# Seven block products in all twelve chunks of tile 7, with the sums of x in two alternating fields

## The chip, the cores and the metric

The kernel runs on one core of a Trainium2 chip. The metric is the device time of one execution in microseconds. Matrix products run on TensorE (PE in the profile), elementwise work on VectorE (DVE), ScalarE (ACT) and GpSimd (POOL); SyncE (SP) issues most DMAs. Each engine works through its own queue in order.

## The reference

Two stages: attention over pooled keys and values, then a gated feed-forward layer on its output.

```python
k_p = k.reshape(B, H, Sp, 8, D).mean(axis=3)          # B=8, H=8, Sp=72, D=64
v_p = v.reshape(B, H, Sp, 8, D).mean(axis=3)
scores = scale * np.matmul(q, k_p.transpose(0, 1, 3, 2))
scores = scores - np.max(scores, axis=-1, keepdims=True)
attn = np.exp(scores)
attn = attn / (np.sum(attn, axis=-1, keepdims=True) + 1e-09)
x = np.matmul(attn, v_p)                              # as 4608 tokens x 512
g = x @ w_gate                                        # 512 x 1536
out = (g * sigmoid(g) * (x @ w_val)) @ w_out          # 1536 x 512
```

## The kernel before

The 4608 tokens of x are cut into nine tiles of 512, numbered 0 to 8, and the 1536 hidden columns into twelve chunks of 128. For every tile and chunk TensorE makes gate and value products into PSUM (gv), ACT and DVE make tanh and products of them (hf), and TensorE adds the chunk's part of the output into four banks (acc, `project`, L956, twelve matmuls). Every operand is held as a high and a low half in 16 bits, so each product is three matmuls.

A chunk's gate and value products come in two forms. The plain form (`side`, L923, lines L927 to L929) takes 24 matmuls of 512 columns. The other form (`product`, L1090, line L1109) splits x and the weights of a chunk into blocks and makes seven block products from sums of blocks, 42 matmuls of 256 columns. It needs the sums of the weights (`fast_weights`, L1014) and the sums of x (`fast_x`, L1045), which DVE, POOL and ACT make beforehand. READY (L65) says for each tile how many chunks, from chunk 0 on, take the seven products; the others of a tile come first, in plain form. MADE (L66) and LATE (L67) say in which tile the sums of a chunk's weights are made.

`fast_x` works in two halves of 256 tokens. Of each half it adds the high and low parts (L1057), makes four differences in the tile `fx` (L1064), casts them to the high halves (ACT, L1077) and subtracts to get the low halves (L1083). A tile whose twelve chunks all take the seven products keeps the first block sum in its own x (L985 to L986); the other tiles keep it in `first`. The other six go to one of two fields of the tensor `area` (`halves_of`, L980): the number of tiles past SOLO (L70), modulo two, says which. The second field lies on the second of the two buffers for softmax numbers (`halves`, L192), so from tile SOLO on `soft` (L816) uses the first buffer alone, and lets a piece wait until TURNS has gone by, in the planner's count, since the transposition of the piece before (L817, L841).

The attention of later tiles runs between the chunks of a tile, in pieces of up to 128 tokens: scores (L631, L632), row maximum and subtraction (L641, L642), exponentials and casts (L653, L713 to L722), POOL's low halves (L727, L730), a transposing DMA (L734), value products (L755, L756), a division (L760), two halves of x (L882, L885) and a transposing DMA into x (L890). Where each step stands on its engine is decided when the program is built, by a planner: `slot` (L1170) lets through what fits beside TensorE's work by its own counts of time. The order on every engine is then fixed. `begin_fast` (L1404) forces what is still missing for a tile's sums before it issues the first product.

CROSS (L69) names the tiles whose first chunk begins inside the last chunk of the tile before (L1475). Then `begin_fast` issues product 5 (which reads the first block sum) and product 1 for the next tile before the output matmuls of the last chunk are all done.

Of the kernel before, what the change touches and what calls it, by code (L numbers as in the profile page):

```python
# [61 lines left out]

ROOM = (3410, 3290)
FAST = 10
READY = (0,0,5,7,9,9,9,9,12)  # L65
MADE = (0,5,7,9,9,9,9,11)  # L66
LATE = {8:(11,)}  # L67
DV = 5
CROSS = (8,)  # L69
SOLO = 7  # L70
CAME = 6000
URGE = (0, 0)
FAST_ROOM = (3500, 1350), (2550, 2210), (1250, 1050), (950, 180), (3350, 800), (1760, 4190), (2900, 5200)
# [27 lines left out]
def attention_then_swiglu(  # L101
# [711 lines left out]
    def soft(t):  # L813

        i, off, b, s0, m = t["at"]
        half, sc = halves[t["me"] % 2 if now["tile"] < SOLO else 0], t["sc"]  # L816
        while now["tile"] >= SOLO and now["pe"] < last["turned"]:  # L817
            yield 0, 0
# [158 lines left out]
    def ready(i):  # L977
        return READY[min(i, len(READY) - 1)]

    def halves_of(i):  # L980

        s = max(0, i - SOLO) % 2
        a = area.bitcast(F16)[:, s * 2 * SLOT : (s + 1) * 2 * SLOT]
# [30 lines left out]
    def fast_weights(c):  # L1014

        yield 1400, 0
        f = xp.tile([P, 2 * DM], F32, name="fw", tag="f", bufs=1)
        g_h, g_l = (a[:, c].rearrange("p i j f -> p (i j f)") for a in (wgv_h, wgv_l))
        nc.vector.tensor_add(f, g_h, g_l)
        a11, a12, a21, a22 = (f[:, i * HT : (i + 1) * HT] for i in range(4))  # L1020
        nc.gpsimd.tensor_add(a22, a21, a22)
        nc.gpsimd.tensor_sub(a21, a11, a21)
        nc.gpsimd.tensor_sub(a11, a22, a11)
        nc.gpsimd.tensor_sub(a12, a12, a11)
        spend("P", 3000, "V")
        yield from settle("P")
        yield 0, 1200
        outs = []
        for places, wgv in zip(sums_of(c), (wgv_h, wgv_l)):
            own = wgv[:, c, 1, :HJ].rearrange("p j f -> p (j f)")  # L1030
            outs.append([*places, (own, slice(3 * HT, 4 * HT))])
        for o, cs in outs[0]:
            nc.scalar.copy(o, f[:, cs])
        for o, cs in outs[1]:
            hi, his = next(q for q in outs[0] if q[1].start <= cs.start < q[1].stop)
            for at in range(cs.start, cs.stop, TILE):
                e = min(cs.stop, at + TILE)
                nc.gpsimd.tensor_sub(
                    o[:, at - cs.start : e - cs.start], f[:, at:e],
                    hi[:, at - his.start : e - his.start],  # L1040
                )
        spend("P", 2600, "A")
        yield from settle("P")
# [46 lines left out]
    def product(o, k, c, i, begin):  # L1090

        x, (rest, one) = xs[i], halves_of(i)
        if k in (3, 6, 7):
            ws = sum_of(c, {3: 1, 6: 0, 7: 2}[k])
        for j in range(HJ):
            w = [a[:, j] for a in ws] if k in (3, 6, 7) else {
                1: (wgv_h[:, c, 0, j], wgv_l[:, c, 0, j]),
                2: (wgv_h[:, c, 0, HJ + j], wgv_l[:, c, 0, HJ + j]),
                4: (wgv_h[:, c, 1, HJ + j], wgv_l[:, c, 1, HJ + j]),
                5: (wgv_h[:, c, 1, j], wgv_l[:, c, 1, j]),  # L1100
            }[k]
            if k in (1, 2, 3):
                rows, cs = {1: (j, slice(0, HT)), 2: (HJ + j, slice(0, HT)), 3: (HJ + j, slice(HT, TILE))}[k]
                xh, xl = x["h"][:, rows, cs], x["l"][:, rows, cs]
            else:
                n = {7: 0, 4: 1, 6: 2}.get(k)
                xh, xl = (a[:, j] for a in one) if n is None else (a[:, j, n] for a in rest)
            for n, (a, b) in enumerate(((w[0], xh), (w[0], xl), (w[1], xh))):
                nc.tensor.matmul(  # L1109
                    o, a, b, start=begin and j + n == 0, stop=j == HJ - 1 and n == 2,  # L1110
                    skip_group_check=True,
                )
                now["pe"] += 109
# [31 lines left out]
    def join(line, g, t=None):  # L1145
        lines[line].append({"g": g, "t": t, "need": next(g)})
# [222 lines left out]
    def hidden_tiles():  # L1369
# [28 lines left out]
        def low_of(eng, hf, hh, n):  # L1398
            hl = hp.tile([P, TILE], BF16, name="hl")
            eng.tensor_sub(hl[:, :n], hf, hh[:, :n].bitcast(F32))  # L1400
            spend(*(("V", 700) if eng is nc.vector else ("P", 1200)), "A")
            return hl

        def begin_fast(k, c):  # L1404
# [11 lines left out]
            product(t["x"], 1, c, k, False)  # L1416
            if c == ready(k) - 1 and SOLO < k + 1 < len(tiles) and ready(k + 1) < NCH and not left[k + 1]:
                summed.add(k + 1)
# [21 lines left out]
        for i, (_, n, _) in list(enumerate(tiles))[1:]:  # L1440
# [15 lines left out]
            if i > 1 and n_fast < NCH and i not in summed:  # L1456
                join("extra", fast_x(i), ("x", i))
                if len(lines["extra"]) > 2:
                    lines["extra"].insert(1, lines["extra"].pop())
            for c in LATE.get(i, ()):  # L1460
                join("extra", fast_weights(c), ("w", c))
# [5 lines left out]
            for at_step, c in enumerate(order):  # L1467
# [5 lines left out]
                if not ends[1] and order[at_step + 1] < n_fast:  # L1473
                    soon = i, order[at_step + 1]
                elif ends[1] and i + 1 in CROSS:  # L1475
                    soon = i + 1, 0
# [41 lines left out]
                else:  # L1518
# [10 lines left out]
                    hl = low_of(nc.gpsimd if i == 1 else nc.vector, h, hh, n)  # L1529
                    if c < MADE[min(i, len(MADE) - 1)]:  # L1530
                        join("extra", fast_weights(c), ("w", c))
# [72 lines left out]
```

## Time and profile before

| | |
|---|---|
| median of 3 runs | 920.8 us (919.76 to 925.22) |
| profiled execution | 923.62 us |
| its span | 921.8 us |
| mean granted TensorE clock | 0.994 of full speed |
| TensorE busy | 886.5 us, 96% of the span |

The span is the time from the first to the last recorded instruction of the profiled execution. Times inside it are given from its start. A row of a timeline has the start, the duration, the engine, the line in the kernel, the operation with what it writes and reads, the shape, how many instructions are merged, and in brackets how long the engine had been idle before and what ended it. The granted clock is a share of full speed, where 1.00 is 2.4 GHz and 0.50 is 1.2 GHz.

### The profile page before, as it was taken

The numbers are of one execution on the slowest core, as the hardware profiler recorded it, in microseconds if no ns is written. First come the engines' busy times: TensorE is split into PE (matmuls) and PEld (weight loads), VectorE is DVE, ScalarE is ACT, GpSimd is POOL, SyncE is SP. The second block draws the span as 40 slices with busy tenths as digits, with TensorE's granted clock in tenths as the row PEclk, the third lists the DMA queues.
The fourth block names the chain that finished last, engine by engine and source line by source line (L and its number), as shares of the span: only waits on it lengthen the run. The fifth ranks groups of instructions, "written<-read, shape, count | busy, mean of one in ns | idle before, by whom it ended". The sixth has DMA issues, their size and how long they took to land.

```text
span 921.8 us, 16917 instructions
## 1 busy us (share of the span) xinstructions
PE 886.5 (96%) x6428; PEld 588.3 (64%) x6519; DVE 646.1 (70%) x1156; ACT 515.7 (56%) x1084; POOL 458.7 (50%) x516
## 2 busy tenths in 40 slices
PE   3889999999999999999999999999999999999997
PEld 3776555454555575567657765776577757777775
DVE  6899997777767679676867777677755585634233
ACT  2677763385456554756476655655647555444343
POOL 3656785498656944776375342543125416114111
PEclk9899999999999999999999999999999999999999
DMA  9866733256444732863285335642333322201001
GB/s 329 264 204 252 255 92 91 77 160 174 84 117 89 202 87 50 203 156 80 53 203 161 77 71 163 169 94 40 84 78 75 76 69 40 31 1 46 1 1 47
DMA packets 161681, 104.76 MB, mean 114 GB/s; under 512 B 119360, under 2 KB 148032, under 8 KB 160064
## 3 DMA queue, kind: packets, MB, share of 16 engines
q1 hardware_dynamic: 159872, 84.81, 36.8%
q10 hardware_dynamic: 1728, 18.88, 5.5%
q8 instruction: 51, 0.84, 0.4%
q14 instruction: 30, 0.25, 0.1%
HBM read 67.63 MB, written 9.44 MB: 84 GB/s over the span
## 4 chain that ended last, share of the span: by engine, by line
PE 74%; DVE 17%; issue 2%; ACT 2%; DMA 2%; POOL 1%; SPq 0%; ACTq 0%; DVEq 0%; POOLq 0%
PE gv L1109 30%; PE acc L963 24%; PE gv L929 5%; PE gv L927 5%; PE gv L928 5%; DVE mixed L244 3%; DVE wgv_l L278 2%; DVE ws L233 2%; DVE hf L945 1%; DVE hf L951 1%; PE ps L631 1%; DMA k<-k_rows 1%; PE ps L416 1%; DVE sc L642 1%; PE ps L632 1%
## 5 line engine op out<-in xcount | busy, mean ns | idle before, releaser
L1400 POOL TENSOR_TENSOR hl<-hf,hh 128x512 bf16<-128x512 f32 x71 | 92.9, 1309 | 201.2 <-ACT hh L1391 201.2
L941 ACT ACTIVATE hf<-gv,un 128x512 f32<-128x512 f32 (+1 forms) x111 | 74.9, 675 | 162.2 <-PE gv L1109 104.3
L963 PE MATMUL acc<-hl,wo_h 128*128 128x512 bf16 (+1 forms) x435 | 161.4, 373 | 2.0
L945 DVE SCALAR_TENSOR_TENSOR hf<-hf,gv 128x512 f32<-128x512 f32 (+1 forms) x111 | 74.4, 670 | 115.4 <-ACT hf L941 115.3
L927 PE MATMUL gv<-x,wgv_h 128*128 128x512 f16 (+1 forms) x408 | 149.7, 367 | 1.9 <-DVE hf L945 1.6
L929 PE MATMUL gv<-x,wgv_l 128*128 128x512 f16 (+1 forms) x408 | 149.7, 367 | 1.6 <-DVE wgv_l L278 1.6
L928 PE MATMUL gv<-x,wgv_h 128*128 128x512 f16 (+1 forms) x408 | 149.6, 367 | 0.0
L963 PE MATMUL acc<-hh,wo_h 128*128 128x512 f32 (+1 forms) x444 | 130.3, 415 | 0.0
L614 POOL TENSOR_TENSOR box<-qt,box 64x512 f16<-64x512 f32 (+1 forms) x60 | 66.3, 1104 | 104.9 <-ACT box L613 91.5
L963 PE MATMUL acc<-hb,wo_l 128*128 128x512 bf16 x307 | 117.4, 382 | 0.4
L1109 PEld LDWEIGHTS <-mixed 128*128 128x128 f16 x1044 | 101.2, 98 | 25.3 <-issue 0.9
L1109 PEld LDWEIGHTS <-wgv_h 128*128 128x128 f16 x960 | 93.0, 98 | 33.7 <-issue 2.0
L1391 ACT CAST hh<-hf 128x512 fp32r<-128x512 f32 x72 | 44.4, 617 | 118.9 <-DVE hf L951 118.7
L1109 PE MATMUL gv<-area,mixed 128*128 128x256 f16 x696 | 95.0, 273 | 0.0
L1109 PE MATMUL gv<-x,wgv_h 128*128 128x256 f16 x528 | 93.0, 273 | 0.0
L951 DVE SCALAR_TENSOR_TENSOR hf<-gv,un,hf 128x512 f32<-128x512 f32 (+1 forms) x87 | 63.2, 727 | 37.6 <-PE gv L1109 34.4
L963 PEld LDWEIGHTS acc<-hh,wo_h 128*128 128x128 f32 x444 | 76.5, 189 | 14.1 <-ACT hh L1391 0.3
L963 PEld LDWEIGHTS <-wo_l 128*128 128x128 bf16 x444 | 43.2, 97 | 52.0 <-issue 26.2
L1109 PE MATMUL gv<-x,wgv_l 128*128 128x256 f16 x264 | 72.0, 273 | 0.0
L929 PEld LDWEIGHTS <-wgv_l 128*128 128x128 f16 x408 | 39.9, 98 | 45.7 <-DVE wgv_l L278 2.9
L928 PEld LDWEIGHTS <-wgv_h 128*128 128x128 f16 x408 | 39.9, 98 | 39.9 <-issue 2.4
L927 PEld LDWEIGHTS <-wgv_h 128*128 128x128 f16 x408 | 39.9, 98 | 37.5
(205 smaller groups left out, 1896.4 us busy)
## 6 DMA issues: line engine op xcount, KB each, us to landing
ws<-w_all ACTq DMA_DIRECT2D x12, 1536.0 KB, 6.7
qt<-q_twice SPq DMA_DIRECT2D x48, 256.0 KB, 3.1
out_t<-ob SPq DMA_DIRECT2D x36, 256.0 KB, 2.5
in<-k_rows SPq DMA_DIRECT2D x12, 576.0 KB, 4.8
in<-q_rows SPq DMA_DIRECT2D x12, 576.0 KB, 4.8
in<-v_main SPq DMA_DIRECT2D x12, 512.0 KB, 4.8
in<-v_rest SPq DMA_DIRECT2D x12, 512.0 KB, 5.0
qt<-q_rows SPq DMA_DIRECT2D x8, 256.0 KB, 4.9
```

Source lines behind the costliest of these rows:

```text
L244: nc.vector.scalar_tensor_tensor(out=wf.bitcast(U32), in0=wf.bitcast(U32), scalar=3, in1=chunks[c]["low"], op0=ALU.logical_shift_left, op1 ...
L614: nc.gpsimd.tensor_sub(o[rows], qt[rows], o[rows])
L927: nc.tensor.matmul(o, wh, x["h"][:, j, a:e], start=(j == 0), stop=False)
L928: nc.tensor.matmul(o, wh, x["l"][:, j, a:e], start=False, stop=False)
L929: nc.tensor.matmul(o, wl, x["h"][:, j, a:e], start=False, stop=(j == NJ - 1))
L941: nc.scalar.activation(hf, gate, AF.Tanh, scale=un[:, c, 0:1])
L945: nc.vector.scalar_tensor_tensor(out=hf, in0=hf, scalar=1.0, in1=gate, op0=ALU.add, op1=ALU.mult)
L951: nc.vector.scalar_tensor_tensor(out=out, in0=val, scalar=un[:, c, 2:3], in1=hf, op0=ALU.mult, op1=ALU.mult)
L963: nc.tensor.matmul(acc[j][:, a:e], w[:, c, j * P : (j + 1) * P], h[:, :n], start=begin and at < NJ, stop=end and w is wo_up,)
L1109: nc.tensor.matmul(o, a, b, start=begin and j + n == 0, stop=j == HJ - 1 and n == 2, skip_group_check=True,)
L1391: nc.scalar.copy(hh[:, :n], hf)
L1400: eng.tensor_sub(hl[:, :n], hf, hh[:, :n].bitcast(F32))
```

## The change

Six constants change. Tile 7 takes seven products in all twelve chunks, as tile 8 does (READY). The sums of weight chunks 9 and 10 are made in tile 6 instead of tile 7 (MADE), those of chunk 11 in tile 7 instead of tile 8 (LATE). Tile 7 begins inside the last chunk of tile 6 (CROSS). SOLO goes from 7 to 6: the sums of x of tile 7 go to the second field and those of tile 8 to the first, and the softmax numbers have one buffer from tile 6 on.

```diff
-READY = (0,0,5,7,9,9,9,9,12)
-MADE = (0,5,7,9,9,9,9,11)
-LATE = {8:(11,)}
+READY = (0,0,5,7,9,9,9,12,12)
+MADE = (0,5,7,9,9,9,11,11)
+LATE = {7:(11,)}
 DV = 5
-CROSS = (8,)
-SOLO = 7
+CROSS = (7,8)
+SOLO = 6
```

On TensorE, where tile 7 starts, the last output matmuls of chunk 7 of tile 6 and what follows them. In both programs x_7737 is x of tile 7, and hl and hb are operands of the output matmuls. Before:

```order
L963 LDWEIGHTS wo_l_110
L963 MATMUL acc3_7904<-hb_8858,wo_l_110 128x512
L963 LDWEIGHTS wo_h_109
L963 MATMUL acc3_7904<-hl_8865,wo_h_109 128x512
L927 LDWEIGHTS wgv_h_107 [waits DMAHW1_49,DMAHW0_49]
L927 MATMUL gv0_8930<-x_7737,wgv_h_107 128x512 [waits PE_49]
L928 LDWEIGHTS wgv_h_107
L928 MATMUL gv0_8930<-x_7737,wgv_h_107 128x512
```

Now:

```order
L963 LDWEIGHTS wo_l_110
L963 MATMUL acc3_7904<-hb_8746,wo_l_110 128x512
L963 LDWEIGHTS wo_h_109
L963 MATMUL acc3_7904<-hl_8753,wo_h_109 128x512
L1109 LDWEIGHTS wgv_h_107 [waits DMAHW3_49,DMAHW0_49]
L1109 MATMUL gv1_8891<-x_7737,wgv_h_107 128x256 [waits Activation_49]
L1109 LDWEIGHTS wgv_h_107
L1109 MATMUL gv1_8891<-x_7737,wgv_h_107 128x256 [waits DVE_49]
```

The first matmul that reads x of tile 7 waited for its DMAs and for a bank of PSUM; it is now one of the block products, and waits for ACT's cast and the next one for DVE's subtraction.

On DVE, the sums of x of tile 7 (fx). Before, the first half's stood after the last products of tile 6 (un_8927 holds factors of tile 7, mt_8946 those of tile 8), the second half's further down:

```order
L951 SCALAR_TENSOR_TENSOR hf_8885<-gv2_8797,un_7719,hf_8885 128x512 [waits DVE_49,PE_49]
L1446 TENSOR_TENSOR un_8927<-p2w_113,mt_7738 128x36
L1057 TENSOR_TENSOR fx_8938<-x_7737 128x2x256 x2
L1064 TENSOR_TENSOR fx_8938<-fx_8938 128x2x128 [waits DVE_49] x4
L908 TENSOR_SCALAR mt_8946<-p2s_121 128x1
```

Now the second half's sums, ahead of the gate of the last chunk of tile 6 (hf_8879 is that chunk's; sc_8295 is the last piece of attention of tile 7, sc_8872 the next piece, of tile 8):

```order
L945 SCALAR_TENSOR_TENSOR hf_8791<-hf_8791,gv0_8725 128x512 [waits Activation_49]
L1492 TENSOR_TENSOR gv1_8686<-gv1_8686,rs_8715 128x256 [waits Activation_49]
L885 SCALAR_TENSOR_TENSOR box_1466<-sc_8295,r_7748,box_1466 64x512 [waits DVE_49]
L951 SCALAR_TENSOR_TENSOR hf_8791<-gv1_8686,un_7719,hf_8791 128x512 [waits DVE_49,PE_49]
L1435 TENSOR_TENSOR gv0_8832<-gv2_8792,rs_8822 128x256 [waits PE_49,Activation_49]
L641 TENSOR_REDUCE mx_8873<-ps_8863 128x4 [waits PE_49]
L642 TENSOR_TENSOR sc_8872<-ps_8863,mx_8873 128x288 [waits DVE_49]
L1057 TENSOR_TENSOR fx_8880<-x_7737 128x2x256 [waits DMAHW3_49,DMAHW0_49]
L1057 TENSOR_TENSOR fx_8880<-x_7737 128x2x256
L1064 TENSOR_TENSOR fx_8880<-fx_8880 128x2x128 [waits DVE_49] x4
L1083 TENSOR_TENSOR x_7737<-fx_8880,x_7737 128x2x128 [waits Activation_49]
L1083 TENSOR_TENSOR area_120<-fx_8880,area_120 128x6x128 [waits Activation_49]
```

All steps of that half now stand in one run, between the scores of the next piece and the gate of the last chunk.

On ACT, a piece's softmax numbers in tile 6. Before, in the second buffer (area):

```order
L941 ACTIVATE hf_8796<-gv0_8754,un_7719 128x512 [waits PE_49,Pool_49]
L1488 COPY gv1_8689<-gv1_8689 128x256 [waits PE_49]
L1424 COPY rs_8827<-gv2_8797 128x256
L713 CAST area_120<-sc_8712 128x8x64 [waits DMAHW4_49,Activation_49]
L1429 COPY gv0_8837<-gv2_8797 128x256 [waits DVE_49]
```

Now in the first (half), as for the piece before it:

```order
L941 ACTIVATE hf_8685<-gv0_8635,un_7719 128x512 [waits PE_49,Pool_49]
L1488 COPY gv2_8591<-gv2_8591 128x256 [waits PE_49,Activation_49]
L1424 COPY rs_8715<-gv1_8686 128x256
L713 CAST half_123<-sc_8515 128x8x64 [waits DMAHW6_49,Activation_49,Pool_49]
L1429 COPY gv0_8725<-gv1_8686 128x256 [waits DVE_49]
```

The cast's place in the chunk is the same; the DMA that it waits for is now that of the piece just before it.

## Rows read from the trace of the kernel before

**Rows 1.** The page, part 1: busy time, share of the span, instructions.

```profile
PE 886.5 (96%) x6428; PEld 588.3 (64%) x6519; DVE 646.1 (70%) x1156; ACT 515.7 (56%) x1084; POOL 458.7 (50%) x516
```

**Rows 2.** Stretches, PE alone: us, PE busy (matmuls), clock, DMA share, GB/s.

```profile
640.00:735.00 95.00, 94.35 (x749) 1.00 0.34 76
```

**Rows 3.** Waits of PE from 640 to 921 us: us, times, longest.

```profile
PE gv L1109 <- DVE hf L951: 0.2, 1, 0.2
```

**Rows 4.** Timeline of PE, a plain chunk of tile 6 and its neighbours.

```profile
657.95 0.20 PE L631 MATMUL ps<-box 128*128 128x72 f16 x1
...
658.20 0.38 PE L927 MATMUL gv<-x,wgv_h 128*128 128x512 f16 x1
...
663.39 0.38 PE L1109 MATMUL gv<-first,wgv_h 128*128 128x256 f16 x2
```

**Rows 5.** Chain that ended last, merged: start, us, what.

```profile
749.42 2.67 PE acc L963 x12
...
822.68 2.62 PE gv L1109 x24
```

**Rows 6.** Timelines of DVE, then ACT, tile 6, around a 64-token piece.

```profile
710.86 0.69 DVE L945 SCALAR_TENSOR_TENSOR hf<-hf,gv 128x512 f32<-128x512 f32 x1 [1.99 <-ACT hf L941]
711.47 0.43 DVE L1492 TENSOR_TENSOR gv<-gv,rs 128x256 f32<-128x256 f32 x1
...
715.14 1.14 DVE L885 SCALAR_TENSOR_TENSOR box<-sc,r,box 64x512 f16<-64x512 f32 x1
716.95 0.46 DVE L641 TENSOR_REDUCE mx<-ps 128x4 f32<-128x288 f32 x1 [0.66 <-PE ps L632]
717.44 0.46 DVE L642 TENSOR_TENSOR sc<-ps,mx 128x288 f32<-128x288 f32 x1
...
710.14 0.69 ACT L941 ACTIVATE hf<-gv,un 128x512 f32<-128x512 f32 x1 [1.43 <-PE gv L1109]
```

**Rows 7.** DMAs into x, issue to landing: at 716 us (at 693 alike); all thirty.

```profile
x<-box SPq DMA_TRANSPOSE x1, 2.6
...
DMA to landing us min/median/max: 2.6/3.4/6.3
```

**Rows 8.** Timelines of DVE, then ACT: sums of x of tile 8; differences of tile 7.

```profile
802.57 1.29 DVE L1057 TENSOR_TENSOR fx<-x 128x512 f32<-128x512 f16 x2
804.71 1.79 DVE L1064 TENSOR_TENSOR fx<-fx 128x256 f32<-128x256 f32 x4
808.68 0.84 DVE L1083 TENSOR_TENSOR x<-fx,x 128x256 f16<-128x256 f32 x1 [0.61 <-ACT x L1077]
...
736.05 2.88 DVE L1064 TENSOR_TENSOR fx<-fx 128x256 f32<-128x256 f32 x4
...
808.25 0.40 ACT L1077 CAST x<-fx 128x256 f16<-128x256 f32 x1
```

**Rows 9.** PE's timeline at three gaps; stretches around them (columns of rows 2).

```profile
20.69 0.16 PE L213 MATMUL ps<-wm,ones 128*128 128x2 bf16 x1 [2.85 <-ACT wgv_h L255]
...
32.61 3.22 PE L416 MATMUL ps<-vr,shapes 128*128 128x128 f32 x16 [1.88 <-DVE p2s L218]
...
478.93 0.20 PE L755 MATMUL ps<-box,pt 128*128 128x64 f16 x1 [1.39 <-DMA pt<-half]
...
19.50:20.00 0.50, 0.00 (x0) 0.60 0.68 207
26.00:27.00 1.00, 1.00 (x9) 0.79 0.67 221
33.00:34.00 1.00, 1.00 (x8) 0.63 1.40 305
36.50:37.00 0.50, 0.50 (x10) 0.83 1.58 272
474.00:479.00 5.00, 3.62 (x25) 1.00 0.69 119
```

**Rows 10.** Transposing DMAs of the softmax numbers (L734): issue to landing, all.

```profile
DMA to landing us min/median/max: 2.8/4.4/6.8
```

## The prediction

> **What bounds the kernel now.** I read the page first: TensorE (PE) is busy 96% of the span, VectorE (DVE) 70%, ScalarE (ACT) 56%, GpSimd (POOL) 50% [rows 1]. Such a share is an average, so I went on to the stage that the change touches, tiles 6 and 7, from about 640 to 830 us. There the table by stretches gives PE 94.35 of the first 95.00 us at the full clock [rows 2], and the list of waits from 640 us to the end holds a single wait of PE on another engine, 0.2 us long [rows 3]. In this stage everything else is hidden beside TensorE. Two things follow: a matmul that goes is gained in full, and a wait that is put in front of TensorE is lost in full.
>
> **What is removed.** Three chunks of tile 7 (9, 10 and 11) change from the plain form to the seven products. The plain form is 24 matmuls of 512 columns. Eight score matmuls start at 657.95 and end with the first plain matmul at 658.20; from there to the next kind at 663.39 the 24 take 5.19 us [rows 4]. The new form is 42 matmuls of 256 columns; 24 of them take 2.62 us, 0.109 each, so 42 take 4.58. The twelve output matmuls are the same in both, 2.67 us [rows 5]. The gain is 0.61 us a chunk, **1.8 us** for three. TensorE is bound there, so nothing gives it back.
>
> **What is added: a wait where tile 7 starts.** Before, tile 7 opened with plain chunks, which need x of tile 7 alone; its sums (first half and second) were made under them. Now the last chunk of tile 6 is followed at once by product 5 of tile 7, whose moving operand is a sum of x over all 512 tokens. So TensorE's own row for it waits for an ACT cast and then for a DVE subtraction of the second half of the sums, and these wait for the last 64-token piece of attention. I count from E, the end of that piece's value matmuls.
>
> TensorE after E: 42 products (4.58 us), 15 output matmuls (15 x 2.67/12 = 3.34) and eight score matmuls (0.25 [rows 4]), so it reaches product 5 at E+8.2. The scores are done three output matmuls earlier, at E+7.5.
>
> The piece's own way: division and scaling go at once, but its low half (L885) stands on DVE behind the chunk's tanh product and the sum of L1492. The tanh waits for 3 output matmuls and 18 products, so it starts at about E+2.8; from tanh to L945 is 0.72, then 0.69, 0.43 and L885 at 0.75 to 1.14: E+5.4 to 5.8 [rows 6]. The transposing DMA of such a 64-row piece took 2.6 us in tile 6 [rows 7], so x is complete at E+8.0 to 8.4.
>
> But DVE has something else ahead of the sums: the row maximum and the subtraction of the next piece's first scores. They wait for the scores at E+7.5, start at about E+7.7 (0.2 for the hand-over is an estimate) and take 0.46 and 0.46, with 0.03 between [rows 6]: E+8.65. Then come, one after the other, two additions (1.29), four differences (1.79), ACT's cast (0.40) and the subtraction into x (0.84), all read from the same steps for tile 8 [rows 8]: 8.65 + 4.32 = E+13.0. Nothing stands between them that TensorE could do. It is ready at E+8.2, may do one matmul of 0.1 us after the cast, and goes on at E+13.0: **4.7 us of idle TensorE**. Queued behind it on PE is all of tile 7. Bounds: 4.0 if the hand-overs overlap by 0.1 us each (L945 starts at 710.86 and takes 0.69, and its follower starts at 711.47 already [rows 6]); 8.1 if the DMA takes the longest 6.3 us of all thirty [rows 7], landing at E+12.1 instead of under the scores; and 1.1 us more if POOL works on SBUF beside the four differences (2.88 instead of 1.79 us at 736.05 [rows 8]). I take 4.7, because the two 64-row landings of tile 6 that I looked at (the DMAs of about 693 and of 716 us) are both 2.6 us.
>
> **The clock after the wait.** TensorE's clock has two levels here, 1.0 and 0.5 in the rows (2.4 and 1.2 GHz). In the kernel's head it idled 2.85 us to 20.69; the clock fell at 19.6 (0.60 over 19.5 to 20.0) and rose at 26.4 (0.79 over 26 to 27). It idled 1.88 us to 32.61; the clock fell at 33.3 (0.63 over 33 to 34) and rose at 36.7 (0.83 over 36.5 to 37). After 1.39 us at 478.93 it stayed at 1.00 [rows 9]. A gap of 4.7 us is longer than both that cost the clock. At half clock the work went on for 5.7 and 3.4 us, half of which is lost: 2.85 and 1.7. I take the middle, **2.3 us**; the ends are 0, if the clock holds, and 2.85.
> The Trainium skill speaks against the change here: the page "TensorE: Matmul & The Clock Gate", section "HAM oscillation — how this bites in real kernels", says that waits for data between bursts of matmuls can throttle the array again, so that the next burst starts cold. By that rule the sum is +5.2 us, without it +2.9; this trace agrees at its two long gaps.
>
> **What moves and costs nothing.** The sums of weight chunks 9 and 10 are made in tile 6 instead of tile 7; TensorE needs them only in the last chunks of tile 7, and the matmuls of tile 6 cover them. The sums of tile 7's first half go into the second field and stand about three chunks before their use. The softmax numbers of tile 6 now share one buffer: a piece's cast (L713) waits for the transposing DMA of the piece before, and behind it on ACT stands the copy that seeds the next gate. Such a DMA took 4.4 us in the median and 6.8 at most [rows 10]; line 817 holds the next piece back by TURNS, 4.5 us by the planner's count. So the cost is 0 at the median and 2.3 at the worst; I take 0. Later pieces of tile 8 are done later in tile 7, but its sums are still ready a chunk before they are used.
>
> **The sum.** -1.8 + 4.7 + 2.3 = **+5.2 us**. The profiled execution took 923.62 us (span 921.80), 2.8 above the median of 920.8; a difference carries over, so the forecast is 920.8 + 5.2 = **926.0 us**.
>
> **Rivals.**
> First, the clock holds through the gap: +2.9, 923.7 us. For it: an idle time of 1.39 us did nothing. Against it: 1.88 and 2.85 did.
> Second, faster: the wait isn't there, because the last piece is finished earlier than I count or the chain overlaps. Then only the gain is left, 919.0 us. Against it: DVE's rows stand in one queue, and its four steps of 4.3 us together cannot fit into the 0.7 us between the scores and product 5.
> Third, slower by over 1%: the last piece's transposing DMA lands late. Place: DVE's wait before the additions. Price: each us beyond about 3 is one more us of idle TensorE. With 2.85 for the clock, it takes -1.8 + 2.85 + 4.7 = 5.75 to start with, and 9.2 is reached when the DMA needs about 6.5 us. For it: 6.3 occurs [rows 7], if POOL also slows the differences that is enough. Against it: the DMA queue is quiet there, and the nearest ones took 2.6.
>
> **Chances.** Forecast (wait and clock) 0.72; clock holds 0.12; no wait 0.06; late DMA 0.09; something unseen that is faster by over 1%, 0.01. A measurement of this kernel can tell about 1% from no change, 911.6 to 930.0 us. So faster 0.01, same 0.90, slower 0.09. The range runs from the case without a wait, 919.0 less half a us for the scatter of a median, to the late DMA, 930.5.
>
> **What would show it.** In the new profile, PE should show one gap of 4 to 5 us before the product matmuls that read x of tile 7, at about 730 to 740 us, released by ACT's cast or DVE's subtraction, and the granted clock at 0.5 for 3 to 6 us behind it; plain matmuls (L927) fall from 408 to 384. DVE's rows before it should read maximum, subtraction, two additions, four differences without a stop. The forecast is wrong if that gap is under 2 us, if the clock stays at 1.00 after it, or if PE waits anywhere else in tiles 6 and 7 for over 1 us.

## The result, and the profile after

The kernel after takes 926.81 us (median of 10 runs, 924.06 to 931.2); the kernel before, run beside it, 921.70 us (10 runs, 919.52 to 925.22). The ratio is 1.0057, with a 95% interval of 1.0036 to 1.0078: 5.1 us more. The forecast was +5.2 us, 926.0.

The page of after, part 1, to be held against [rows 1]:

```profile
PE 884.0 (96%) x6481; PEld 591.5 (64%) x6573; DVE 640.1 (69%) x1159; ACT 518.7 (56%) x1093; POOL 461.0 (50%) x519
```

TensorE (PE) has less to do (884.0 instead of 886.5 us) and the program is slower: the time has gone into waiting and, as the stretches show, into work at a lower clock. The stretches, PE alone, in the columns of [rows 2]:

```profile
640.00:735.00 95.00, 90.77 (x708) 0.96 0.29 65
735.00:830.00 95.00, 93.53 (x761) 1.00 0.21 45
```

In [rows 2] the first of them had 94.35 us busy at 1.00. Now 3.6 us of work and 0.04 of the clock are missing there. The list of waits of PE from 640 us to the end, where [rows 3] had a single line of 0.2 us:

```profile
PE gv L1109 <- ACT x L1077: 2.5, 1, 2.5
PE gv L1109 <- DVE x L1083: 1.0, 1, 1.0
PE acc L963 <- POOL hl L1400: 0.6, 1, 0.6
PE gv L1109 <- DVE hf L951: 0.4, 2, 0.2
```

The first two are the wait that was forecast, at the first product of tile 7. PE's timeline there:

```profile
724.77 0.38 PE L963 MATMUL acc<-hl,wo_h 128*128 128x512 bf16 x1
727.65 0.27 PE L1109 MATMUL gv<-x,wgv_h 128*128 128x256 f16 x1 [2.50 <-ACT x L1077]
728.93 0.37 PE L1109 MATMUL gv<-x,wgv_h 128*128 128x256 f16 x1 [1.01 <-DVE x L1083]
```

Output matmuls follow one another here every 0.22 us, so PE was ready at 724.99 and went on in earnest at 728.93, with one matmul of 0.11 between: 3.8 us idle. (The brackets, 2.50 and 1.01, add up to 3.5, because they count from the modelled end of a matmul and not from where the next one could have started.) What it waited for, on DVE and then on ACT:

```profile
724.69 0.45 DVE L641 TENSOR_REDUCE mx<-ps 128x4 f32<-128x288 f32 x1
725.17 0.46 DVE L642 TENSOR_TENSOR sc<-ps,mx 128x288 f32<-128x288 f32 x1
725.55 1.28 DVE L1057 TENSOR_TENSOR fx<-x 128x512 f32<-128x512 f16 x2
726.75 1.80 DVE L1064 TENSOR_TENSOR fx<-fx 128x256 f32<-128x256 f32 x4
728.46 0.42 DVE L1083 TENSOR_TENSOR x<-fx,x 128x256 f16<-128x256 f32 x1
...
727.20 0.41 ACT L1077 CAST x<-fx 128x256 f16<-128x256 f32 x1 [2.74 <-DVE fx L1064]
```

Maximum, subtraction, additions, differences and subtraction stand without a stop, and PE goes on 0.05 us after the last of them ends (728.88). The granted clock around the gap (columns as above):

```profile
726.00:728.00 2.00, 0.27 (x1) 0.96 0.00 0
728.00:730.00 2.00, 1.07 (x6) 0.50 0.00 0
...
732.00:734.00 2.00, 2.00 (x11) 0.50 0.00 0
734.00:735.00 1.00, 1.00 (x6) 0.66 0.00 0
735.00:736.00 1.00, 0.93 (x5) 1.00 0.00 0
```

It falls to 0.50 (1.2 GHz) in the idle time, and the share of 0.66 from 734 to 735 puts its rise at 734.7. Work ran from 728.93 to there at half clock, 5.75 us, of which half, 2.9 us, is lost.

**A yardstick.** The spans of the two profiled executions, 921.8 and 922.0 us, do not show this. The head of the kernel differs from run to run: tile 6 begins at 640.78 us in before, at 635.46 in after. So every kernel below is measured inside its own profiled execution, from the row that begins tile 6 (DVE's `un`, L1446) to the start of DVE's last store copy (L1120; in some experiments both stand a few lines further down). These are the two rows of before, then those of after:

```profile
640.78 0.19 DVE L1446 TENSOR_TENSOR un<-p2w,mt 128x36 f32<-128x36 f32 x1
916.96 0.69 DVE L1120 COPY ob<-acc 128x512 f32<-128x512 f32 x1 [0.17 <-PE acc L963]
```

```profile
635.46 0.19 DVE L1446 TENSOR_TENSOR un<-p2w,mt 128x36 f32<-128x36 f32 x1
917.15 0.69 DVE L1120 COPY ob<-acc 128x512 f32<-128x512 f32 x1 [0.17 <-PE acc L963]
```

276.18 us before, 281.69 after: +5.51. The parts found above add up to it: -1.83 (three chunks, 3 x 0.61) + 3.8 (idle) + 2.9 (clock) + 0.6 (a wait for `hl`, from the list) = +5.5.

### The profile page after: what moved, and what is told of

Same layout as the page of the kernel before. It is cut to its first block, busy times and chain, and to the rows that moved or that the text cites. A ratio compares the mean times of both kernels' runs of the same rounds, so it can differ in the third digit from the quotient of the medians.

```text
span 922.0 us, 17043 instructions
## 1 busy us (share of the span) xinstructions
PE 884.0 (96%) x6481; PEld 591.5 (64%) x6573; DVE 640.1 (69%) x1159; ACT 518.7 (56%) x1093; POOL 461.0 (50%) x519
## 4 chain that ended last, share of the span: by engine, by line
PE 71%; DVE 15%; DMA 4%; ACT 3%; POOL 3%; issue 3%; SPq 0%; DVEq 0%; ACTq 0%; POOLq 0%
PE gv L1109 30%; PE acc L963 23%; PE gv L929 5%; PE gv L927 5%; PE gv L928 5%; DVE mixed L244 2%; DVE wgv_l L278 2%; DVE hf L945 1%; DVE hf L951 1%; DMA k<-k_rows 1%; DMA pt<-area 1%; PE ps L631 1%; DMA ws<-w_all 1%; DVE fx L1057 1%; PE ps L632 1%
## 5 line engine op out<-in xcount | busy, mean ns | idle before, releaser
L1400 POOL TENSOR_TENSOR hl<-hf,hh 128x512 bf16<-128x512 f32 x74 | 96.7, 1307 | 217.2 <-ACT hh L1391 217.1
L927 PE MATMUL gv<-x,wgv_h 128*128 128x512 f16 (+1 forms) x384 | 140.5, 366 | 1.8 <-DVE hf L945 1.5
L929 PE MATMUL gv<-x,wgv_l 128*128 128x512 f16 (+1 forms) x384 | 140.4, 366 | 1.4 <-DVE wgv_l L278 1.4
L928 PE MATMUL gv<-x,wgv_h 128*128 128x512 f16 (+1 forms) x384 | 140.4, 366 | 0.0
L1109 PEld LDWEIGHTS <-wgv_h 128*128 128x128 f16 x1008 | 98.1, 98 | 39.4 <-issue 5.1
L614 POOL TENSOR_TENSOR box<-qt,box 64x512 f16<-64x512 f32 (+1 forms) x60 | 66.1, 1101 | 98.4 <-ACT box L613 86.0
L1109 PE MATMUL gv<-x,wgv_h 128*128 128x256 f16 x600 | 106.2, 274 | 3.7 <-ACT x L1077 2.5
L1109 PE MATMUL gv<-area,mixed 128*128 128x256 f16 x708 | 97.3, 274 | 0.0
L951 DVE SCALAR_TENSOR_TENSOR hf<-gv,un,hf 128x512 f32<-128x512 f32 (+1 forms) x90 | 65.4, 727 | 37.1 <-PE gv L1109 34.0
L1109 PE MATMUL gv<-x,wgv_l 128*128 128x256 f16 x300 | 82.4, 275 | 0.0
L929 PEld LDWEIGHTS <-wgv_l 128*128 128x128 f16 x384 | 37.5, 98 | 42.7 <-DVE wgv_l L278 2.7
L928 PEld LDWEIGHTS <-wgv_h 128*128 128x128 f16 x384 | 37.6, 98 | 37.3 <-issue 2.4
L1435 DVE TENSOR_TENSOR gv<-gv,rs 128x256 f32<-128x256 f32 x63 | 27.1, 430 | 48.9 <-PE gv L1109 43.3
```

The lines of the kernel that those rows point to most:

```text
L614: nc.gpsimd.tensor_sub(o[rows], qt[rows], o[rows])
L927: nc.tensor.matmul(o, wh, x["h"][:, j, a:e], start=(j == 0), stop=False)
L928: nc.tensor.matmul(o, wh, x["l"][:, j, a:e], start=False, stop=False)
L929: nc.tensor.matmul(o, wl, x["h"][:, j, a:e], start=False, stop=(j == NJ - 1))
L951: nc.vector.scalar_tensor_tensor(out=out, in0=val, scalar=un[:, c, 2:3], in1=hf, op0=ALU.mult, op1=ALU.mult)
L1109: nc.tensor.matmul(o, a, b, start=begin and j + n == 0, stop=j == HJ - 1 and n == 2, skip_group_check=True,)
```

## The experiments

The theory to be tested: the wait for the second half of tile 7's sums of x, and the half clock behind it, outweigh a gain that is really there. Against it stand the edits that were priced at nothing (one softmax buffer, sums of weights moved to tile 6) and a gain smaller than counted. "The stage" is the time from tile 6's start to the last store copy, in one profiled execution of each kernel.

| kernel | from, to (us) | stage | against before | ratio in the timed runs |
|---|---|---|---|---|
| before | 640.78, 916.96 | 276.18 | | |
| before, second execution | 637.35, 913.55 | 276.20 | 0.0 | |
| after | 635.46, 917.15 | 281.69 | +5.5 | 1.0057 [1.0036, 1.0078] |
| after, second execution | 641.32, 921.65 | 280.33 | +4.1 | |
| 1 sums a chunk earlier | 640.87, 925.54 | 284.67 | +8.5 | 1.0098 [1.0082, 1.0115] |
| 2 filled gap | 639.01, 917.99 | 278.98 | +2.8 | 1.0040 [1.0027, 1.0052] |
| 3 the rest alone | 637.76, 913.86 | 276.10 | -0.1 | 1.0013 [0.9997, 1.0029] |
| 4 eleven chunks | 637.74, 918.75 | 281.01 | +4.8 | 1.0088 [1.0058, 1.0119] |
| 5 split start | 639.43, 919.56 | 280.13 | +3.9 | 1.0047 [1.0032, 1.0063] |
| 6 no crossing | 642.64, 925.13 | 282.49 | +6.3 | 1.0081 [1.0058, 1.0104] |
| 7 turns of 7000 | 649.80, 932.82 | 283.02 | +6.8 | 1.0185 [1.0162, 1.0208] |
| 8 interleaved | 638.37, 916.50 | 278.13 | +1.9 | 1.0031 [1.0009, 1.0053] |
| 9 copy first | 640.99, 916.79 | 275.80 | -0.4 | 0.9997 [0.9971, 1.0023] |
| 11 low half first | 641.09, 915.66 | 274.57 | -1.6 | 0.9976 [0.9958, 0.9995] |

**Are the readings a property of the kernel?** Both kernels were profiled a second time, unchanged.

> The kernel before, unchanged, as a second look at the yardstick: 276.2 us from tile 6's start to the last store copy, within 0.3, if it is a property of the kernel; between 275 and 278 if it scatters from run to run.

> The kernel after, unchanged, as a second look. If the time from tile 6's start to the last store copy is a property of the kernel and not of the run, it repeats: 281.7 us within 0.3, with the wait at line 1109 of 2.5 and 1.0 us and half clock behind it for 5 to 6 us. If it is scatter of the run, it comes out elsewhere between 276 and 284.

Before repeats within 0.02 us. After came out at 280.33, 1.36 less than in its first execution, and so outside the 0.3 us that were expected: its two waits are the same to 0.01 us (2.51 and 1.01), but the clock comes back sooner. Work began at 734.80 in this run; the stretches, PE alone:

```profile
736.00:737.00 1.00, 1.00 (x7) 0.50 0.00 0
737.00:738.00 1.00, 1.00 (x14) 0.63 0.00 0
738.00:739.00 1.00, 1.00 (x12) 1.00 0.00 0
```

0.63 puts the rise at 737.7: 2.9 us at half clock, 1.5 lost, where the first execution lost 2.9. That accounts for the difference. So the wait belongs to the kernel, and the price of the clock behind it was 1.4 us apart in two executions. A stage with a fall of the clock in it is known no better than that.

**The clock alone (2).** The gap is filled with work whose result is overwritten:

```diff
+            if (k, c) == (7, 0):
+                for _ in range(18):
+                    nc.tensor.matmul(val, wgv_h[:, 0, 0, 0], xs[6]["h"][:, 0], start=True, stop=True, skip_group_check=True)
             product(t["r"], 5, c, k, True)
```

> The kernel after with 18 matmuls of 512 columns (18 x 0.216 = 3.9 us, their result is overwritten) put before product 5 of tile 7's first chunk, so that TensorE works through the wait. Theory (the wait itself costs 3.8 us, the clock behind it 2.9 us): the wait stays as work that nobody needs, the clock stays at 1.00 from 640 us on, the time is 2.9 us under the kernel after, about 924, ratio to before 1.0025. Rival (the clock's fall costs nothing, since TensorE isn't what bounds the start of tile 7): as the kernel after, ratio 1.0055, with 2 to 3 us of new waits on PE in the 10 us behind the start of tile 7.

PE's timeline and the stretch around it:

```profile
728.54 4.05 PE L1417 MATMUL gv<-x,wgv_h 128*128 128x512 f16 x18
732.42 0.38 PE L1109 MATMUL gv<-x,wgv_h 128*128 128x256 f16 x2
...
720.00:740.00 20.00, 20.00 (x163) 1.00 0.21 42
```

The sums are ready as late as ever: DVE's subtraction starts at 732.01 and takes 0.42, so the fill only just covers the wait and the gap's length is kept. The clock stays at 1.00, and the stage is 2.7 us shorter than in after's first execution and 1.4 shorter than in its second, close to the 2.9 and 1.5 us that the clock took there. The rival, that half clock costs nothing there, is out: there is no new wait of 2 to 3 us behind tile 7's start, only the one for `hl` (0.4 us), which after has too. The timed ratio fell as well (1.0040), but its interval overlaps that of after; it is the stage that shows it.

**What was priced at nothing (3).** The kernel before with one softmax buffer from tile 6 and the sums of weight chunks 9 and 10 in tile 6, nothing else. Those sums replace blocks that the plain chunks 9 and 10 of tile 7 read, so the values of these two chunks are not the reference's; every instruction runs as it would.

```diff
-MADE = (0,5,7,9,9,9,9,11)
+MADE = (0,5,7,9,9,9,11,11)
-        half, sc = halves[t["me"] % 2 if now["tile"] < SOLO else 0], t["sc"]
-        while now["tile"] >= SOLO and now["pe"] < last["turned"]:
+        half, sc = halves[t["me"] % 2 if now["tile"] < 6 else 0], t["sc"]
+        while now["tile"] >= 6 and now["pe"] < last["turned"]:
```

> The kernel before with only what was costed at nothing: one buffer of softmax numbers from tile 6 on, and the sums of weight chunks 9 and 10 made in tile 6. Tile 7 keeps three plain chunks first. Theory: no change, ratio to before 1.000 within 0.0007, no wait of PE over 1 us from 640 us on. Rival (these two cost up to the 2.3 us of the transposing DMA's worst case, or more): ratio 1.0015 to 1.003, with the wait of PE on an engine of the attention work in tile 6 or 7.

276.10 against 276.18 us: nothing. PE's only wait from 640 us on is the 0.2 us of [rows 3]. The timed ratio, 1.0013 with an interval of 0.9997 to 1.0029, would not tell theory from rival; the stage does. The sums of weight chunk 11, which after makes in tile 7, are not part of this test.

**Three ways to take the wait away that failed (1, 4, 6).** Experiment 1 makes the sums of weights 9 and 10 in tile 7 again, and the planner then places the sums of x earlier.

```diff
-MADE = (0,5,7,9,9,9,11,11)
-LATE = {7:(11,)}
+MADE = (0,5,7,9,9,9,9,11)
+LATE = {7:(9,10,11)}
```

> The kernel after, but the sums of weight chunks 9 and 10 are made in tile 7 again, so the planner puts the second half of tile 7's sums of x one chunk earlier, ahead of product 5 by a chunk. Theory (TensorE waits for these sums at tile 7's start, 3.8 us in the trace of after, and works 5.75 us at half clock behind that wait): wait and clock go together, the gain of three chunks stays: 1.8 us under the kernel before, ratio to before 0.998, about 920; no wait of PE over 1 us on line 1109, granted clock 1.00 from 640 us to tile 8. Rival 1 (the single buffer of the softmax numbers costs, which stays here): at or above the kernel before, ratio 1.000 or more, though line 1109 shows no wait. Rival 2 (the sums only get in one another's way elsewhere): the wait on line 1109 is gone and another engine's wait of 2 to 4 us stands on PE in tile 7.

A miss, and the slowest of the three. Its waits of PE:

```profile
PE gv L1109 <- DVE gv L1492: 4.7, 2, 4.3
PE gv L1109 <- DVE x L1083: 1.3, 1, 1.3
PE gv L1109 <- ACT x L1077: 0.8, 1, 0.8
```

The wait at tile 7's start shrank from 3.5 to 2.1 us but did not go: the additions ran a chunk earlier, yet the steps after them had to queue behind the softmax casts on ACT and softmax rows on DVE, after which the subtraction stands (732.95). One of these rows, L664, took 1.21 us, to 732.79, where it took 0.17 in after; POOL was at work on a low half (L1400) until 732.77. And a new wait of 4.3 us came in the middle of tile 7. PE waits there for DVE's sum (L1492), DVE for ACT's tanh, and ACT for this:

```profile
778.98 0.62 ACT L713 CAST half<-sc 128x512 f16<-128x512 f32 x1 [5.93 <-DMA pt<-half]
```

The cast into the one softmax buffer waits for the transposing DMA of the piece before, with the tanh (779.84) queued behind it. That DMA was issued late. POOL, then the DMA queue:

```profile
772.42 0.67 POOL L1038 TENSOR_TENSOR wgv_l<-fw,wgv_h 128x256 f16<-128x256 f32 x1
773.05 1.15 POOL L727 TENSOR_TENSOR half<-sc,half 128x512 f16<-128x512 f32 x1
774.16 0.45 POOL L730 TENSOR_TENSOR half<-sc,half 128x32 f16<-128x32 f32 x2
...
774.64 1.32 SPq L734 DMA_TRANSPOSE pt<-half  x1
```

The low halves of the piece (L727, L730), which the DMA needs, stand on POOL right behind low halves of a weight chunk's sums (L1038, from 770.67), and the DMA lands 4.2 us after its issue. So the wait of 4.3 us, and the second fall of the clock behind it, come from the one buffer and from the weight sums on POOL together. In after's order the buffer cost nothing.

Experiment 7 was to test the part of the buffer by keeping pieces farther apart (`TURNS` 7000 for 4500).

> The first experiment's kernel with 7000 in place of 4500 as the planner's distance between two pieces in the one softmax buffer. In its trace ACT's cast into that buffer waited 5.93 us for the transposing DMA of the piece before, the tanh behind it came late, and PE waited 4.3 us in tile 7. Theory: that wait goes with its clock loss, the wait at tile 7's start stays as in the first experiment (0.8 + 1.3 us): 284.7 less 4 to 7 us, 278 to 281 us from tile 6's start to the last store copy. Rival (the wait isn't from the buffer but from three sums of weights in tile 7): 284 to 285 us with the same wait.

Inconclusive. The wait for L1492 is gone, as the theory has it, but the number moves more than this distance: tile 6 begins only at 649.8 us, and the sums of x are late again (PE waits 4.8 and 0.9 us for them at tile 7's start, and 0.7 us for those of tile 8). Its rival, the weight sums, is not out: in experiment 1's rows they are part of the cause.

Experiment 4 puts one plain chunk in front of tile 7, which needs no sums:

```diff
-READY = (0,0,5,7,9,9,9,12,12)
+READY = (0,0,5,7,9,9,9,11,12)
-LATE = {7:(11,)}
+LATE = {8:(11,)}
-CROSS = (7,8)
+CROSS = (8,)
```

> The kernel after with eleven chunks of tile 7 by seven products and chunk 11 plain, first in the tile; single softmax buffer and weight sums of 9 and 10 in tile 6 as in after. Theory: a plain chunk needs x alone, not its sums, so it covers the making of the sums (24 matmuls, 5.19 us, against a wait of 3.8 us); two chunks are gained, 2 x 0.61 = 1.2 us: ratio to before 0.9987, about 920.5, no wait over 1 us at line 1109. Rival 1 (the plain chunk only moves the wait, as DVE and ACT are the bound in these chunks): a wait of 1 to 3 us at line 1109 one chunk later, ratio 1.000 to 1.003. Rival 2 (seven products gain less than counted): ratio 1.000 without any wait.

Rival 1 holds in kind: the wait moved one chunk on. Its size is 4.1 us, more than the 1 to 3 of the rival and the 3.5 of after's list:

```profile
PE gv L1109 <- ACT first L1077: 3.6, 1, 3.6
PE gv L1109 <- DVE first L1083: 0.5, 1, 0.5
```

The data were not late here. The last piece of x had landed at 719.0 (its DMA was issued at 713.90 and took 5.1 us), but the order put the second half's additions behind the plain chunk's gate, and ACT's cast behind that chunk's own casts. DVE, then ACT:

```profile
736.77 1.28 DVE L1057 TENSOR_TENSOR fx<-x 128x512 f32<-128x512 f16 x2
...
740.95 0.59 ACT L1394 CAST hb<-gv 128x512 bf16<-128x512 f32 x1
741.43 0.42 ACT L1077 CAST first<-fx 128x256 f16<-128x256 f32 x1
```

Experiment 6 leaves tile 7 out of `CROSS`, so chunk 11 of tile 6 ends first:

```diff
-CROSS = (7,8)
+CROSS = (8,)
```

> The kernel after, but the last chunk of tile 6 ends before tile 7's first product starts (one number: tile 7 leaves the list of tiles begun across the border). Products 3, 7 and 4 of chunk 11 and the output of chunk 10, 1.95 + 2.67 = 4.6 us of TensorE, then stand in front of product 5. Theory: the sums are ready (wait of 3.8 us covered), the clock holds; the price is a wait for the chunk's own hh and for the copies that seed tile 7's first gate, 1 to 2 us: from tile 6's start to the last store copy 275.5 to 276.5 us, ratio to before 0.9995 to 1.0005. Rival (the sums move back with TensorE's order, since the planner makes them late): a wait of 2 us or more on line 1109 for x as in after, 279 us or more.

The rival holds again. PE comes to product 5 later, and DVE's additions start later still, at 737.88, behind all of chunk 11's own steps, so PE waits 3.83 and 1.01 us, longer than in after, and 1.25 us later on for a sum of L1492. The additions also took 2.35 us in place of after's 1.28, while POOL worked on L614 and L1400 (to 739.67): the slowdown beside POOL that the prediction had priced at 1.1 us, for the differences, as a bound. In both experiments PE work put in front of the reader did not cover the sums, because they moved back with it; in 6 they follow directly on the row that begins tile 7, as `begin_fast` forces out what is still missing only when its product's turn has come.

**Moving work past the wait by hand (5, 8, 9, 11).** These write out the order of PE at the border: product 1, which reads plain x of the first half, opens tile 7; the last chunk's products 3, 7, 4 and nine output matmuls follow; then products 2, 5 and 6 of tile 7.

```diff
-            product(t["r"], 5, c, k, True)
-            product(t["x"], 1, c, k, False)
+            if not split:
+                product(t["r"], 5, c, k, True)
+            product(t["x"], 1, c, k, split)
...
         def second_fast(t, k, c, split=False):
+            if split:
+                product(t["gate"][:, :HT], 2, c, k, False)
+                product(t["r"], 5, c, k, False)
+                keep_fast(t)
             product(t["x"], 6, c, k, False)
```

> The kernel after, but the first chunk of tile 7 starts with product 1 (it reads plain x of the first half), and products 2 and 5 come behind the last chunk's products 3, 7 and 4 and nine of its twelve output matmuls, product 6 behind them. In the trace of after TensorE is ready for product 5 at 725.0 and the operand is ready at 728.9; the moved work (products 1, 3, 7, 4 and 2, 5 x 0.65, and nine output matmuls, 9 x 0.22) is 5.2 us. Theory: the wait of 3.8 us and the clock's 2.9 us go, the gain of 1.8 us stays: from tile 6's start to the last store copy 274.4 us (before 276.2, after 281.7), ratio to before 0.998. Rival (DVE and ACT set the end of this chunk, their queue stands behind the sums): 1 to 4 us of waits on PE for the tanh, the gate or hl of that chunk, 276 to 280 us.

The wait for x is gone, and the rival's stands in its place, with 0.6 us more on a copy of ACT behind it (L1499 is L1492 of the other kernels, seven lines having come in above it):

```profile
736.18 0.59 PE L1109 MATMUL gv<-area,wgv_h 128*128 128x256 f16 x2 [3.22 <-DVE gv L1499]
```

PE has passed the sums by, but chunk 11's own sum on DVE (735.70, 0.42 us) stands behind them in DVE's queue, and product 4 needs it. The clock fell again.

Experiment 8 therefore splits the sums on DVE as well: additions and two differences, then chunk 11's two steps, then the rest. On PE it also puts product 6 behind the last output matmuls.

```diff
+                if on is nc.vector and i == 7 and n and at:
+                    now["part"] = True
+                    while not now.get("rest"):
+                        yield 0, 0
...
+                    if split:
+                        seed_fast(new)
+                        now["rest"] = True
+                        while any(e["t"] == ("x", 7) for e in lines["extra"]):
+                            forward("extra", {"V": 1e9, "A": 1e9})
```

> The kernel after with the order around tile 7's start written out on PE and DVE. PE: product 1 of tile 7, then products 3 and 7 of chunk 11, seven output matmuls, product 4, two output matmuls, products 2 and 5 of tile 7, three output matmuls, product 6. DVE: additions and two differences of the sums, then chunk 11's own gate product (L945) and sum, and only then the other two differences and the two subtractions. Theory, from the times of after: the sum of chunk 11 on DVE ends at 728.7, so product 4 waits 0.3 us; the sums of x end at 730.5 and 731.9, where PE comes to their readers at 730.6 and 731.9. So no wait over 1.4 us, the clock stays at 1.00 from tile 6 on, the three chunks' gain stays: 1.8 us less 0.3 to 0.9 of small waits, from tile 6's start to the last store copy 274.7 to 275.3 us (before 276.2, after 281.7), ratio to before 0.9985 to 0.999. Rival (ACT and the attention pieces pushed back by this order decide): a wait of 1.5 to 4 us on a hh, hl or gate copy of chunk 11 or of tile 7's first chunk, a fall of the clock behind it, 277 to 281 us.

Half a hit. The sums are covered, the clock holds, and PE's list has no wait at product 4, where 0.3 us were worked out (the list's 0.3 us for L1506 stand at 804.51, well into tile 7). The largest wait left, 2.2 us, is on a copy (L1429) that stands on ACT behind two preparations of queries and two casts; 0.8 us for a transposed softmax piece and 0.4 for `hl` come after it. Here and in 9 and 11 the products are line 1113, and L1429, L1506 and L1404 are L1424, L1492 and L1400 of after. PE, then ACT, then the stretch:

```profile
737.13 0.81 PE L1113 MATMUL gv<-area,mixed 128*128 128x256 f16 x6 [2.21 <-ACT rs L1429]
...
733.03 0.72 ACT L611 ACTIVATE qt<-qt,inv 128x512 f32<-128x512 f32 x1
...
736.71 0.36 ACT L1429 COPY rs<-gv 128x256 f32<-128x256 f32 x1
...
735.00:740.00 5.00, 2.87 (x39) 1.00 0.39 107
```

Experiment 9 puts that copy first, and chunk 11's later steps (`rest_of_chunk`: L951, its casts, `hl`) behind it:

```diff
                         product(t["r"], 4, c, i, False)
-                        times_val(hf, hf, t["val"], un, c)
+                        if not split:
+                            rest_of_chunk()
...
                             second_fast(new, *soon, split)
+                            if split:
+                                rest_of_chunk()
```

> The kernel of the experiment before, with chunk 11's last steps (L951, its casts to hh and hb, the scores of the next piece and the preparation of queries) put behind tile 7's product 5 and the copy of its result on ACT, which had stood behind two query preparations and two casts (733.03 to 736.71) and made PE wait 2.2 us for product 6. Theory: that wait goes, as the copy follows product 5 at once (734.1 + 0.2 + 0.4, before PE's 735.2): 278.1 less 2.2, 275.9 us from tile 6's start to the last store copy, 275.0 if the wait of 0.8 us for a transposed piece goes too; ratio to before 0.9985 to 1.000. Rival (the work put off comes back as a wait of the next chunks on ACT, hl or the attention piece): the 2.2 us reappear within 20 us behind the tile's start, 277.5 us or more.

The 2.2 us are gone, and of the work put off 1.1 us come back, in kind as the rival said and half of its size, on POOL, where `hl` stands behind the low halves of two query pieces. PE, then POOL:

```profile
743.63 0.38 PE L963 MATMUL acc<-hl,wo_h 128*128 128x512 bf16 x1 [1.14 <-POOL hl L1404]
...
739.96 2.39 POOL L614 TENSOR_TENSOR box<-qt,box 64x512 f16<-64x512 f32 x2 [9.11 <-ACT box L613]
742.31 1.26 POOL L1404 TENSOR_TENSOR hl<-hf,hh 128x512 bf16<-128x512 f32 x1
```

Experiment 11 exchanges these two on POOL:

```diff
-                        slot(*FAST_ROOM[6])
+                        if not split:
+                            slot(*FAST_ROOM[6])
                         pending.append((acc, *ends, i, c, hh, hb, low_of(nc.vector if final else nc.gpsimd, hf, hh, n)))
+                        if split:
+                            slot(*FAST_ROOM[6])
```

> The kernel of the experiment before, with one more step exchanged on POOL: chunk 11's hl goes ahead of the low halves of the next queries (L614, 2.39 us), behind which it stood from 739.96 to 742.31 while PE waited 1.14 us for it. Theory: hl is done about 2 us before its reader, the wait goes, and the three chunks' gain is left with small waits only: 275.8 less 1.1, 274.7 us from tile 6's start to the last store copy (before 276.2), no wait of PE over 0.5 us there, ratio to before 0.998 to 0.999, which may not be told from 1 in the times. Rival (the queries come late instead): a wait of about 1 us on the scores or on ACT for the next piece, 275.5 to 276.5 us.

All of PE's waits from 600 us to the end, and the stretch of tile 7:

```profile
PE gv L1113 <- DVE gv L1506: 0.3, 1, 0.3
PE gv L1113 <- DVE hf L951: 0.2, 1, 0.2
...
735.00:830.00 95.00, 94.04 (x779) 1.00 0.20 46
```

The stage is 274.57 us, 1.6 under before, and the timed ratio, 0.9976 with an interval of 0.9958 to 0.9995, lies under 1, if barely: this version is faster than before by about 0.2% (medians of 921.04 and 922.57 us), and its stage is the shortest of the table. The gain of three chunks, 1.8 us, is what is left when next to nothing waits.

## Why the prediction was right

- **The gain of 1.8 us.** Shown by experiment 11: -1.6 us of stage with 0.3 us of new wait (at 810.92, well into tile 7), where 3 x 0.61 less 0.3 is -1.5.
- **The wait.** Its place in the program, its two releasers and its mechanism were as forecast; it stands at 725 us and not at 730 to 740, as tile 6 began 5.3 us earlier in this execution than in before's. The end of the last piece's value matmuls, E, was 716.9 in this run. PE was ready at 725.0 (E+8.1; forecast 8.2), and the additions began at 725.55 (E+8.65, as forecast). Only the last stretch was over-sized: 4.7 us forecast, 3.8 measured. ACT's cast starts at 727.20, before all the differences are done, where the sum took it behind them, and the subtraction took 0.42 us where [rows 8] had 0.84. (That one ran in before while POOL was at work on L1400, from 807.96 to 809.23; in after POOL stood idle from 725.34 to 735.87.) In place of 4.32 us the chain took 3.33 (725.55 to 728.88).
- **The clock.** Forecast 2.3 us with bounds of 0 and 2.85. After's two executions lost 2.9 and 1.5, and the stage with the gap filled was 2.7 and 1.4 us shorter than theirs. The head had shown 5.7 and 3.4 us of work at half clock ([rows 9]); here it was 5.75 and 2.9. Taking the middle was right for the two together, and right for neither.
- **What was to cost nothing** cost nothing in before's order: experiment 3, -0.1 us.
- **What was not seen:** 0.6 us of wait for `hl`, 0.4 in the second execution. POOL does it in tile 7 behind the sums of weight chunk 11 and a softmax low half. That these sums move into tile 7 is part of the change, and the prediction has no term for it. The wait is within the 1 us that the prediction allowed elsewhere.
- **A bound that was too narrow.** The single softmax buffer was given 2.3 us at the worst, by the longest transposing DMA less the planner's distance. In experiment 1 ACT waited 5.93 us for that DMA and PE 4.3. The DMA itself took 4.2 us; what the bound left out is POOL, whose weight sums held back the DMA's issue.

In the first execution the under-sized clock, the unseen 0.6 and the over-sized wait nearly cancel (+0.6, +0.6, -0.9), which gives 5.5; in the second the clock was over-sized as well (-0.8, +0.4, -0.9), and the stage grew by 4.1. The timed runs, +5.1, lie between. That the total was hit within 0.1 us is luck of that kind; the terms themselves were right to within 1 us each.

Of the rivals, "the clock holds" is out by its row of 0.50, "no wait" by its two lines of the list, and the late DMA by the additions that began right behind DVE's subtraction.

## What to carry to other kernels

In this kernel a product that needs data made by other engines met its wait at the border of a tile, where the chain that makes the data starts with the previous stage's last result: count that chain instruction by instruction from there, and compare it with what the matmul engine still has to do. To put work into such a gap it was not enough here to reorder the waiting engine; the same exchange was due on every queue that serves both sides of the border (DVE, then ACT, then POOL), and each one left out showed up as the next wait (3.2, 2.2 and 1.1 us). Where a head scatters by several us from run to run, a stage measured between two rows of one execution resolves a few tenths, as long as the clock does not fall in it.

## What the runs showed of the hardware that was not expected

The same gap does not always cost the same clock. After's two executions have equal waits, and then half clock for 5.75 us of work in the one and 2.9 in the other. In experiment 8 PE sat idle for 2.21 us in tile 7, and the granted clock stayed at 1.00 in every stretch from 640 to 840 us, whereas 1.88 us of idleness in the head had brought it down ([rows 9]), and so had the waits of 0.81 and 1.29 us at tile 7's start in experiment 1 (0.57 over 733 to 734, then 0.50). The rule of the Trainium skill that the prediction cited (the page "TensorE: Matmul & The Clock Gate", section "HAM oscillation — how this bites in real kernels", that waits between bursts can throttle the array again) agrees with after and with experiments 1, 4, 5, 6 and 7, and the gap of experiment 8 is a case where a wait did not. What sets the difference, none of these runs shows.
